# One level of Strassen's scheme for the last matrix product of a fused retention and MLP kernel

## The chip, the cores and the metric

The kernel runs on one core of one Trainium2 chip. The metric is the device time of one launch in microseconds (us), as the median of several runs. A core has five engines that run side by side, each with its own instruction queue that it works off in order: PE (TensorE, the matrix multiplier; PEld is its weight load), DVE (VectorE), ACT (ScalarE), POOL (GpSimd) and SP (SyncE, which here only issues DMAs). SBUF is the on-chip memory. PSUM is the memory that PE writes its products to; this kernel uses it as eight banks of 128 partitions by 512 float32 numbers.

## The reference: what is computed

Two layers follow each other. The first is a recurrent retention over 4 batches, 8 heads, 768 steps and a head size of 64; the second is an MLP over its 3072 rows.

```python
def _attn_ref(q, k, v):
    ...
    for t in range(S):
        state = gamma[None, :, None, None] * state + np.einsum('bhd,bhe->bhde', k[:, :, t], v[:, :, t])
        y[:, :, t] = scale * np.einsum('bhd,bhde->bhe', q[:, :, t], state)

def _moe_ref(x, w_in, w_out):     # x: 3072 x 512, w_in: 512 x 2048, w_out: 2048 x 512
    h = x @ w_in
    g = h * np.cos(h)
    return (g @ w_out).astype(np.float32)
```

All matmuls of the kernel take bf16 operands and add up in float32.

## The kernel before

**Tiles and stages.** The sequence is cut into chunks of 128 steps. A pair `p` (0 to 11) is one chunk of two batches, so 256 rows of the MLP. Two pairs make a group `g` (0 to 5) of 512 rows. For each pair there is a block: `y_block(p)`, many small matmuls that make the retention's output `y` of this pair, bring its state `st_ps` up to date and make the score matrices of pair `p + 1`. Behind it stand the block's copies: `y_copy` (two of them, ACT, to `xt`), `s_copy` (the state from PSUM to the bf16 tile `stb`) and four `a_mask` (DVE, scores times mask, to `am`). For each group there are two large products. The first, here called F, is `f_mm(g, f)` for 16 row blocks `f` of the hidden layer: four matmuls of 512 columns each into one bank; then `f_cos` (ACT, the cosine into one of three `cosb` tiles), then `f_mul` (DVE, h times cos(h), into row `f` of `gt[g % 2]`). The second, here called O, is `o_mm(g, j, part)`: for each of the four row tiles `j` of 128 rows there are 16 matmuls of 512 columns, in four parts, that take `gt` as weights and `w_out_sb` as the moving operand and add up in one bank; then `o_out` (ACT, to one of four `ob` tiles) and `o_dma` (SP, a 256 KB write).

**Order.** Groups 0 and 1 and pairs 0 to 6 are placed by a planner with given costs (`Plan`); the change doesn't touch it. From group 2 on the order is written out by hand (L946 to L970). A group has 16 steps `s`. Step `s` of group `g` issues F of block `s` of this group, and beside it one part of O of the group before. At steps 3 and 11 a block follows, with its copies and `conv` (ACT and POOL bring `q`, `k`, `v` of pair `p + 2` to bf16, SP transposes them by DMA), and SP issues loads. Blocks exist in groups 2, 3 and 4 (pairs 6 to 11). The pass `g == NG` is the end: it holds O of group 5 alone, with the last row tile split into 384 and 128 columns (`last_o`).

**What is shared.** Seven PSUM banks go round in a first-in, first-out list (`Banks`): `f_mm`, `o_mm` and `y_block` (six banks: two for `y`, four for the scores) take from its head, and the program hands a bank back where its last reader is issued. PE waits on the chip until that reader is done. Between the halves of a block one other engine passes a signal on (`told`, `hop_on`, L531); from pair 6 on this is POOL. `PRE` is 5: the float32 loads `qf`, `kf`, `vf` have five buffers each, and pair `p` uses number `p % 5`.

Of the kernel before, what the change touches and what calls it, by code (L numbers as in the profile page):

```python
# [9 lines left out]
FP32 = mybir.dt.float32  # L10
BF16 = mybir.dt.bfloat16
AF = mybir.ActivationFunctionType
ALU = mybir.AluOpType
# [160 lines left out]
def kernel(  # L174
# [9 lines left out]
    nc = tc.nc  # L184
    B, H, S, D = q.shape
    C = 128
    NC = S // C
    DM = H * D
# [3 lines left out]
    KOUT = DF // 128  # L192
    NP = B // 2 * NC
    NG = NP // 2
# [4 lines left out]
    ORDER = [0, NC] + [x for x in range(1, NP) if x != NC]  # L199
# [25 lines left out]
    w_out_sb = sb([128, KOUT, DM], BF16, "w_out_sb")  # L225
    qf = [sb([128, 2, H, D], FP32, f"qf{i}") for i in range(PRE)]
    kf = [sb([128, 2, H, D], FP32, f"kf{i}") for i in range(PRE)]
    vf = [sb([128, 2, H, D], FP32, f"vf{i}") for i in range(PRE)]
    ob = [sb([128, DM], FP32, f"ob{i}") for i in range(4)]
# [7 lines left out]
    xt = [sb([128, KIN, 4 * C], BF16, f"xt{i}") for i in range(2)]  # L237
    gt = [sb([128, KOUT, 4 * C], BF16, f"gt{i}") for i in range(2)]
    cosb = [sb([128, 4 * C], BF16, f"cosb{i}") for i in range(3)]
    kx = sb([128, H, 2, D], BF16, "kx")  # L240
    vx = sb([128, 2, H, D], BF16, "vx")
    mask = [sb([128, 128], BF16, f"mask{i}") for i in range(2)]
# [11 lines left out]
    far = gtf[:, 4352:4608].bitcast(FP32)  # L254

    amf = [gtf[:, 5120 + 1024 * i : 6144 + 1024 * i].bitcast(FP32) for i in range(2)]

    def by_b(t, p):

# [15 lines left out]
    def load(eng, p, names):  # L275

        bp, c = divmod(ORDER[p], NC)
        for n in names.split():  # L280
            t, src = SRC[n[0].lower()]
            if len(n) == 1:
                t = (qb(p) if n == "Q" else kb(p)) if n in "QK" else t[p % PRE]
                eng.dma_start(  # L284
                    out=t.rearrange("p b h d -> p (b h) d"),
                    in_=src[ds(2 * bp, 2), :, ds(c * C, C), :].rearrange(
                        "b h t d -> t (b h) d"))
            elif n[1] == "s":
# [23 lines left out]
    ENG = {"D": nc.vector, "P": nc.gpsimd}  # L312

    def copy(e, out, in_):
        if e == "A":
            nc.scalar.copy(out=out, in_=in_)  # L316
        else:
            ENG[e].tensor_copy(out=out, in_=in_)  # L318
# [37 lines left out]
    held = {}  # L356
# [228 lines left out]
    def s_copy(p, e):  # L585
        copy(e, stb[(max(p, 1) + 1) % 2], st_ps)
# [3 lines left out]
    def f_mm(g, f):  # L590
        bank = held["f", g, f] = banks.take()
        for i in range(KIN):
            nc.tensor.matmul(bank, lhsT=w_in_sb[:, i, ts(f, 128)], rhs=xt[g % 2][:, i, :],  # L593
                             start=(i == 0), stop=(i == KIN - 1))

    def f_cos(key):
        cb = cosb[f_no[0] % 3]
        f_no[0] += 1
        bank = held[key]
        held[key] = (bank, cb)  # L600
        nc.scalar.activation(out=cb, in_=bank, func=AF.Sin, bias=halfpi)  # L601

    def f_mul(g, f):
        bank, cb = held["f", g, f]
        nc.vector.tensor_tensor(out=gt[g % 2][:, f, :], in0=bank, in1=cb, op=ALU.mult)  # L605
        banks.give(bank)
# [20 lines left out]
    o_no = [0]  # L627

    def o_row(g, j):
        bp, c = divmod(ORDER[2 * g + j // 2], NC)  # L630
        return (2 * bp + j % 2) * S + c * C

    def o_mm(g, j, part):
        if part == 0:
            held["o", g, j] = banks.take()
        bank = held["o", g, j]
        for f in range(4 * part, 4 * part + 4):
            nc.tensor.matmul(bank, lhsT=gt[g % 2][:, f, ts(j, 128)], rhs=w_out_sb[:, f, :],  # L638
                             start=(f == 0), stop=(f == KOUT - 1))

    def o_out(g, j, e):
        bank = held["o", g, j]
        o = ob[o_no[0] % 4]
        o_no[0] += 1
        copy(e, o, bank)
        banks.give(bank)
        held["dma", g, j] = o

    def o_dma(g, j):
        nc.sync.dma_start(out=out[ds(o_row(g, j), C), :], in_=held.pop(("dma", g, j)))  # L650

    def last_o(g, j):

        o = ob[o_no[0] % 4]
        for i, (lo, n) in enumerate(((0, 384), (384, 128))):
            bank = banks.take()
            for f in range(KOUT):
                nc.tensor.matmul(bank[:, :n], lhsT=gt[g % 2][:, f, ts(j, 128)],  # L658
                                 rhs=w_out_sb[:, f, ds(lo, n)],
                                 start=(f == 0), stop=(f == KOUT - 1))  # L660
            copy("AD"[i], o[:, ds(lo, n)], bank[:, :n])
            (nc.sync, nc.scalar)[i].dma_start(
                out=out[ds(o_row(g, j), C), ds(lo, n)], in_=o[:, ds(lo, n)])

    def idle_mm(e, n=1):
        bank = banks.take()
# [19 lines left out]
        out=dist.rearrange("p (a b) -> p a b", a=8),  # L686
        in0=far[:, :8].unsqueeze(2).to_broadcast([128, 8, 16]),
        in1=far[:, 8:24].unsqueeze(1).to_broadcast([128, 8, 16]), op=ALU.add)
# [31 lines left out]
    at = lambda tm: dict(start=0.0, free=0.0, done=tm, lat=0.0)  # L720
# [30 lines left out]
    for p in range(PL + 2):  # L751
        c = ORDER[p] % NC
# [120 lines left out]
        for u in units:  # L873
            f = u[2]
# [49 lines left out]
    def block(p):  # L924
        nxt = p + 1 < NP
        y_block(p, nxt)
        for b in range(2):
            y_copy(p, b, "A")
        if has_s(p):
            s_copy(p, "D")  # L930
        if nxt:
            for u in range(2):
                for b in range(2):
                    a_mask(p + 1, b, u)

    def conv(p):
        for b in range(2):
            conv_k(p, b, "A")
        for b in range(2):
            conv_q(p, b, "P")  # L940
        for b in range(2):
            conv_v(p, b, "P")
        for w in (1, 0):
            dma_t(p, w)

    for g in range(2, NG + 1):  # L946
        for s in range(16):
            hf, r = divmod(s, 8)
            p = 2 * (g + 1) + hf
            if g < NG:  # L950
                if g == 2 and s == 0:
                    o_mm(1, 0, 0)
                f_mm(g, s)
                f_cos(("f", g, s))
                f_mul(g, s)
            if g == NG and s == 12:
                last_o(NG - 1, 3)
                break
            if g > 2 or s > 0:
                o_mm(g - 1, *divmod(s, 4))  # L960
            if s % 4 == 3:
                o_out(g - 1, s // 4, "A")
            if p < NP and r == 3:
                block(p)
            if s % 4 == 3:
                o_dma(g - 1, s // 4)
            if p + 2 < NP and r == 3:
                conv(p + 2)
            if p + 3 < NP and s % 4 == 3:
                load(nc.sync, p + 3, "q ks" if r == 3 else "vs")  # L970


# [28 lines left out]
```

## Time and profile before

| what | value |
|---|---|
| median of three runs (lowest to highest) | 209.26 us (208.71 to 209.42) |
| span of the profiled execution, first to last instruction | 206.6 us |
| difference of the two, which lies around the span | 2.7 us |
| PE busy | 201.9 us, 98% of the span |
| DVE busy | 112.9 us, 55% |
| ACT busy | 115.1 us, 56% |
| POOL busy | 75.2 us, 36% |
| granted TensorE clock, mean | 1.000 |
| written to and read from HBM | 6.29 MB and 27.26 MB |

The profile is of one execution; the page gives its span, and no separate device time for it. A row of a group gives the line, the engine, the operation, output and inputs with their shapes, the count, the busy time and the mean duration of one. A duration is longer than the distance between two starts where instructions overlap, as matmuls do. A row of the timeline gives start, duration, engine, line and count of a run of like instructions. Group 2's hand-written steps start at about 69.6 us, those of group 3 at 101.2 us, of group 4 at 131.8 us, of group 5 at 161.9 us, and the end at 188.7 us.

### The profile page before, as it was taken

What the parts mean: (1) busy time and instruction counts of PE and PEld (TensorE: products, weight loads), DVE (VectorE), ACT (ScalarE), POOL (GpSimd) and SP (SyncE); (2) the same over time, 40 slices, a digit from 0 to 9 for tenths busy, and PEclk for the clock granted to TensorE, in tenths of its full rate; (3) what the DMA queues carried; (4) which work ended last, traced back from release to release, by engine and by line L of the source; (5) the groups of instructions that cost most, each with busy time, mean ns of one, the idle gap of its engine ahead of it and who ended that gap; (6) DMA issues with size and microseconds to landing.
All of it is one profiled execution on the core that took longest, in us unless ns stands there. A gap on an engine that the chain in (4) does not pass through costs nothing.

```text
span 206.6 us, 5235 instructions
## 1 busy us (share of the span) xinstructions
PE 201.9 (98%) x2179; PEld 108.9 (53%) x2179; DVE 112.9 (55%) x194; ACT 115.1 (56%) x193; POOL 75.2 (36%) x79
## 2 busy tenths in 40 slices
PE   7999999999999999999999999999999999999994
PEld 2547665868945545445445445445444444444442
DVE  5477899776787548338438438448442444444000
ACT  7566794859965357547547546554555553554120
POOL 8899989799985003305206105200000000000000
PEclk9999999999999999999999999999999999999999
DMA  6999999999999865886876975501101101110212
GB/s 117 172 264 201 304 242 322 252 333 278 341 332 190 199 156 150 206 210 155 190 183 157 144 198 147 156 0 56 53 1 51 51 3 51 51 51 0 105 52 102
DMA packets 59656, 32.15 MB, mean 156 GB/s; under 512 B 48752, under 2 KB 54128, under 8 KB 59632
## 3 DMA queue, kind: packets, MB, share of 16 engines
q0 software_dynamic: 15408, 15.47, 34.6%
q1 hardware_dynamic: 44080, 16.28, 31.7%
q8 instruction: 17, 0.28, 0.6%
q10 hardware_dynamic: 144, 0.07, 0.1%
q14 instruction: 7, 0.06, 0.1%
HBM read 27.26 MB, written 6.29 MB: 162 GB/s over the span
## 4 chain that ended last, share of the span: by engine, by line
PE 93%; DMA 4%; POOL 1%; issue 0%; DVE 0%; POOLq 0%; DVEq 0%
PE bank L638 39%; PE bank L593 30%; PE bank L614 10%; DMA kx<-in_k_dram 4%; PE bank L392 2%; PE bank L483 2%; PE bank L364 2%; PE bank L658 2%; PE st_ps L511 2%; PE bank L667 2%; PE bank L497 1%; POOL ks L284 1%; PE bank L434 1%; POOL qs L284 1%; PE bank L402 0%
## 5 line engine op out<-in xcount | busy, mean ns | idle before, releaser
L601 ACT ACTIVATE cosb<-bank,halfpi 128x512 bf16<-128x512 f32 x96 | 65.6, 689 | 54.1 <-PE bank L593 47.8
L638 PE MATMUL bank<-w_out_sb,gt 128*128 128x512 bf16 x368 | 91.0, 379 | 0.0
L605 DVE TENSOR_TENSOR gt<-bank,cosb 128x512 bf16<-128x512 f32 x72 | 49.1, 689 | 55.7 <-ACT cosb L601 55.7
L593 PE MATMUL bank<-xt,w_in_sb 128*128 128x512 bf16 x288 | 73.2, 379 | 0.0
L638 PEld LDWEIGHTS <-gt 128*128 128x128 bf16 x368 | 35.5, 98 | 42.3 <-DMA w_out_sb<-in_moe_w_out_dram 0.3
L593 PEld LDWEIGHTS <-w_in_sb 128*128 128x128 bf16 x288 | 27.5, 98 | 32.3
L327 POOL TENSOR_TENSOR qs<-qf,gq 128x512 bf16<-128x512 f32 x18 | 18.5, 1046 | 42.4 <-PE bank L483 32.0
L411 DVE TENSOR_TENSOR am<-bank,mask 128x512 bf16<-128x512 f32 x40 | 24.8, 681 | 3.5 <-PE bank L392 3.5
L316 ACT COPY ob<-bank 128x512 f32<-128x512 f32 (+1 forms) x24 | 14.0, 582 | 16.0 <-PE bank L638 13.9
L614 PE MATMUL bank<-xt,w_in_sb 128*128 128x256 bf16 x192 | 22.4, 273 | 0.0
L614 PEld LDWEIGHTS <-w_in_sb 128*128 128x128 bf16 x192 | 18.6, 98 | 3.3 <-DVE xt L318 0.3
L622 DVE TENSOR_TENSOR gt<-bank,cosb 128x512 bf16<-128x512 f32 x24 | 16.2, 689 | 5.6 <-ACT cosb L601 5.4
L316 ACT CAST xt<-bank 128x512 bf16<-128x512 f32 x21 | 11.4, 588 | 10.6 <-PE bank L483 10.5
L316 ACT CAST ks<-kf 128x512 bf16<-128x512 f32 x20 | 11.5, 623 | 1.9 <-DMA kf<-in_k_dram 1.9
L667 PE MATMUL bank<-zero 128*128 128x512 bf16 x35 | 11.2, 449 | 1.1 <-DVE halfpi L683 1.1
L483 PE MATMUL bank<-am,vs 64*64 64x128 bf16 (+1 forms) x320 | 10.3, 206 | 0.1
L334 POOL TENSOR_TENSOR vs<-vf,gk 128x512 bf16<-128x512 f32 x8 | 8.2, 1043 | 6.0 <-DMA vf<-in_v_dram 3.8
L284 POOL DMA_DIRECT2D vf<-in_v_dram x8 | 9.4, 1178 | 1.9 <-DVE vs L339 1.4
L339 POOL TENSOR_TENSOR vs<-vf,gk 128x512 bf16<-128x512 f32 x8 | 8.7, 1096 | 2.5 <-PE bank L483 1.3
L318 DVE CAST stb<-st_ps 128x512 bf16<-128x512 f32 x9 | 6.2, 689 | 3.4 <-PE st_ps L511 2.6
L483 PEld LDWEIGHTS <-vs 64*64 64x64 bf16 x320 | 7.8, 107 | 0.5 <-POOLq L531 0.2
L392 PE MATMUL bank<-qkt 64*64 64x128 bf16 (+1 forms) x320 | 7.9, 206 | 0.0
(66 smaller groups left out, 131.7 us busy)
## 6 DMA issues: line engine op xcount, KB each, us to landing
out_dram<-ob SPq DMA_DIRECT2D x23, 256.0 KB, 2.5
vf<-in_v_dram POOLq DMA_DIRECT2D x8, 512.0 KB, 11.7
qf<-in_q_dram POOLq DMA_DIRECT2D x6, 512.0 KB, 12.3
kf<-in_k_dram POOLq DMA_DIRECT2D x6, 512.0 KB, 12.1
w_out_sb<-in_moe_w_out_dram POOLq DMA_DIRECT2D x4, 512.0 KB, 14.1
qf<-in_q_dram SPq DMA_DIRECT2D x4, 512.0 KB, 4.8
w_in_sb<-in_moe_w_in_dram POOLq DMA_DIRECT2D x5, 256.0 KB, 8.5
kf<-in_k_dram SPq DMA_DIRECT2D x16, 64.0 KB, 3.1
```

The lines of the kernel that those rows point to most:

```text
L284: eng.dma_start(out=t.rearrange("p b h d -> p (b h) d"), in_=src[ds(2 * bp, 2), :, ds(c * C, C), :].rearrange("b h t d -> t (b h) d"))
L316: nc.scalar.copy(out=out, in_=in_)
L327: ENG[e].tensor_tensor(out=qb(p)[:, b], in0=qf[p % PRE][:, b], in1=bc(gq, ORDER[p] % NC), op=ALU.mult)
L411: nc.vector.tensor_tensor(out=am[p % 2][b][u], in0=bank.rearrange("p (a t) -> p a t", a=HP), in1=(dec[:, b] if p < 2 else mask[second(p, 0 ...
L483: m = nc.tensor.matmul(held["yp", p][b][ts(j, 64), a, lo:], lhsT=vs[p % NB][ts(r, 64), b, h, :], rhs=am[p % 2][b][h // 4][ts(r, 64), h % 4 ...
L593: nc.tensor.matmul(bank, lhsT=w_in_sb[:, i, ts(f, 128)], rhs=xt[g % 2][:, i, :], start=(i == 0), stop=(i == KIN - 1))
L601: nc.scalar.activation(out=cb, in_=bank, func=AF.Sin, bias=halfpi)
L605: nc.vector.tensor_tensor(out=gt[g % 2][:, f, :], in0=bank, in1=cb, op=ALU.mult)
L614: nc.tensor.matmul(bank[:, ts(e, 256)], lhsT=w_in_sb[:, i, ts(f + e, 128)], rhs=xt[g % 2][:, i, ts(hf, 256)], start=(i == 0 and e == 0), s ...
L622: nc.vector.tensor_tensor(out=gt[g % 2][:, f : f + 2, ts(hf, 256)], in0=bank.rearrange("p (f t) -> p f t", f=2), in1=cb.rearrange("p (f t) ...
L638: nc.tensor.matmul(bank, lhsT=gt[g % 2][:, f, ts(j, 128)], rhs=w_out_sb[:, f, :], start=(f == 0), stop=(f == KOUT - 1))
L667: nc.tensor.matmul(bank[:, : 256 * n].rearrange("p (n t) -> p n t", n=n), lhsT=zero[:, :128], rhs=zero.unsqueeze(1).to_broadcast([128, n, ...
```

## The change

O of groups 2 to 5 is done by one level of Strassen's scheme in the form with seven products and sums that are used again. The group's hidden matrix is split into halves by rows (pairs `2g` and `2g + 1`) and by the hidden index (blocks 0 to 7 and 8 to 15), and `w_out` by the hidden index and by columns (256 each). Each of the seven products is, for both batches `j`, eight matmuls of 256 columns. DVE and POOL make the operand sums: of `w_out` once, in group 2 (`w_sum`, T1 to T4), and of `gt` in every group (`g_sum`, S1 to S4), each in two halves of 1024 bf16 elements per partition. S1, S2, S4 and T1, T2, T3 lie in load buffers 2 and 3 of `qf`, `kf` and `vf`; S3 overwrites its operand in `gt`. The partial results are added up by DVE from PSUM (`add_up`, float32), with one copy by ACT ahead, and are written by four DMAs per group in runs of 1 KB (`c_dma`). F's blocks are issued in the order 0, 8, 1, 9 and so on. `s_copy` of the hand-written blocks moves from DVE to ACT. `last_o` goes.

```diff
+    T4 = sb([128, KOUT // 2, DM // 2], BF16, "T4")
+    part1 = [sb([128, 2, DM // 2], FP32, f"part{i}") for i in range(2)]
...
+    T1, T2, T3 = (halves(t[2]) for t in (qf, kf, vf))
+    S1, S2, S4 = (halves(t[3]) for t in (qf, kf, vf))
...
-    def last_o(g, j):
...
+    def w_sum(n, e, x):
+        k = ts(x, HK // 2)
+        out, a, b, op = {
+            1: (T1, w_quad(0, 1), w_quad(0, 0), ALU.subtract),
+            2: (T2, w_quad(1, 1), T1, ALU.subtract),
+            3: (T3, w_quad(1, 1), w_quad(0, 1), ALU.subtract),
+            4: (T4, w_quad(1, 0), T2, ALU.subtract)}[n]
+        ENG[e].tensor_tensor(out=out[:, k], in0=a[:, k], in1=b[:, k], op=op)
+
+    def g_sum(g, n, e, x, of=2):
+        k = ts(x, HK // of)
+        t = gt[g % 2]
+        out, a, b, op = {
+            1: (S1, quad(t, 1, 0), quad(t, 1, 1), ALU.add),
+            2: (S2, S1, quad(t, 0, 0), ALU.subtract),
+            3: (quad(t, 1, 0), quad(t, 0, 0), quad(t, 1, 0), ALU.subtract),
+            4: (S4, quad(t, 0, 1), S2, ALU.subtract)}[n]
+        ENG[e].tensor_tensor(out=out[:, k], in0=a[:, k], in1=b[:, k], op=op)
+
+    def product(g, n, j, on=None):
+        t = gt[g % 2]
+        a, b = {
+            1: (quad(t, 0, 0), w_quad(0, 0)), 2: (quad(t, 0, 1), w_quad(1, 0)),
+            3: (S4, w_quad(1, 1)), 4: (quad(t, 1, 1), T4),
+            5: (S1, T1), 6: (S2, T2), 7: (quad(t, 1, 0), T3)}[n]
...
+        for k in range(HK):
+            nc.tensor.matmul(bank[:, ts(j, HM2)], lhsT=a[:, k, ts(j, 128)], rhs=b[:, k, :],
+                             start=(on is None and j == 0 and k == 0), stop=(k == HK - 1),
+                             skip_group_check=True)
...
+    def add_up(out, n, other, js=slice(0, 2)):
+        nc.vector.tensor_tensor(out=out[:, js], in0=pbank(n)[:, js], in1=other[:, js], op=ALU.add)
...
         if has_s(p):
-            s_copy(p, "D")
+            s_copy(p, "A")
...
+    def o_step(g, s):
+        if s in (0, 1):
+            product(g, 1, s)
+            if s == 1:
+                nc.scalar.copy(out=pu[0], in_=pbank(1))
+        elif s == 3:
+            for j in range(2):
+                product(g, 2, j, on=1)
+            O[0, 0] = new_ob()
+            nc.scalar.copy(out=O[0, 0], in_=pbank(2))
+            put(2)
+        elif s in (4, 5):
+            product(g, 6, s - 4)
+            if s == 5:
+                add_up(pu[1], 6, pu[0])
+                put(6)
+        elif s in (6, 7):
...
+        elif s in (8, 9):
+            product(g, 5, s - 8)
...
+        elif s == 11:
+            for j in range(2):
+                product(g, 3, j, on=5)
+            O[0, 1] = new_ob()
+            add_up(O[0, 1], 3, pu[1])
+            put(3)
+        elif s in (12, 13):
+            product(g, 4, s - 12)
+            if s == 13:
+                O[1, 0] = new_ob()
+                add_up(O[1, 0], 4, pu[0])
+                put(4)
+
+    def sums(g, s):
+        x = 0 if s >= 12 else 1
+        n = (1, 2, 4, 3)[s % 4]
+        if n != 4:
+            g_sum(g - x, n, "D", x)
+
+    def pool_sums(g, s):
+        if s == 3:
+            if 2 <= g - 1 < NG:
+                g_sum(g - 1, 4, "P", 1)
+        elif s == 15 and g < NG:
+            g_sum(g, 4, "P", 0)
...
-    for g in range(2, NG + 1):
+    for g in range(2, NG):
         for s in range(16):
             hf, r = divmod(s, 8)
             p = 2 * (g + 1) + hf
+            f = s // 2 + 8 * (s % 2)
...
+            f_mm(g, f)
+            f_cos(("f", g, f))
+            if s < 4 and g > 2 or s >= 12:
+                sums(g, s)
+            f_mul(g, f)
+            if g > 2:
+                o_step(g - 1, s)
+            else:
...
+                if s in (4, 5, 8, 9):
+                    w_sum(1 + s // 8, "D", s % 2)
             if p < NP and r == 3:
                 block(p)
...
+            if g == 2 and r == 3:
+                for x in range(2):
+                    w_sum(3 + s // 8, "P", x)
+            pool_sums(g, s)
...
+    g = NG - 1
+    for n in (1, 2):
+        g_sum(g, n, "D", 1)
+    g_sum(g, 4, "P", 1)
+    g_sum(g, 3, "D", 1)
+    for j in range(2):
+        product(g, 1, j)
+    nc.scalar.copy(out=pu[0], in_=pbank(1))
+    for j in range(2):
+        product(g, 4, j)
...
+    o = new_ob()
+    for j in range(2):
+        product(g, 3, j)
+        add_up(o, 3, pu[1], slice(j, j + 1))
+        c_dma(g, 0, 1, o, (nc.sync, nc.scalar)[j], slice(j, j + 1))
```

More of the change, by code (lines that the diff above doesn't have):

```diff
@@ L256, with halves @@
     amf = [gtf[:, 5120 + 1024 * i : 6144 + 1024 * i].bitcast(FP32) for i in range(2)]
+    def halves(t):
+        return t.rearrange("p b h d -> p (b h d)").bitcast(BF16).rearrange(
+            "p (f m) -> p f m", f=KOUT // 2)
+    T1, T2, T3 = (halves(t[2]) for t in (qf, kf, vf))
+    S1, S2, S4 = (halves(t[3]) for t in (qf, kf, vf))
     def by_b(t, p):
@@ L650, in o_dma @@
         nc.sync.dma_start(out=out[ds(o_row(g, j), C), :], in_=held.pop(("dma", g, j)))
-    def last_o(g, j):
[L654 to L663, printed above, removed]
+    HK, HM2 = KOUT // 2, DM // 2
@@ new lines, in quad, with w_quad @@
+    def quad(t, r, c):
+        return t[:, ts(c, HK), ts(r, HM2)]
+    def w_quad(r, c):
+        return w_out_sb[:, ts(r, HK), ts(c, HM2)]
+    def w_sum(n, e, x):
[6 more added lines that the diff above has]
+        ENG[e].tensor_tensor(out=out[:, k], in0=a[:, k], in1=b[:, k], op=op)
@@ new lines, in g_sum @@
+    def g_sum(g, n, e, x, of=2):
[13 more added lines that the diff above has]
+            5: (S1, T1), 6: (S2, T2), 7: (quad(t, 1, 0), T3)}[n]
+        if on is None and j == 0:
+            held["P", n] = banks.take()
+        elif on is not None:
+            held["P", n] = held["P", on]
+        bank = held["P", n]
+        for k in range(HK):
+            nc.tensor.matmul(bank[:, ts(j, HM2)], lhsT=a[:, k, ts(j, 128)], rhs=b[:, k, :],
+                             start=(on is None and j == 0 and k == 0), stop=(k == HK - 1),
+                             skip_group_check=True)
@@ new lines, in put, with pbank, new_ob, c_dma @@
+    def put(n):
+        banks.give(held["P", n])
+    def pbank(n):
+        return held["P", n].rearrange("p (j m) -> p j m", j=2)
+    def new_ob():
+        o_no[0] += 1
+        return ob[(o_no[0] - 1) % 4].rearrange("p (j m) -> p j m", j=2)
+    def add_up(out, n, other, js=slice(0, 2)):
+        nc.vector.tensor_tensor(out=out[:, js], in0=pbank(n)[:, js], in1=other[:, js], op=ALU.add)
+    def c_dma(g, r, c, o, eng=None, js=None):
+        bp, ch = divmod(ORDER[2 * g + r], NC)
+        rows = out.rearrange("(b s) m -> s b m", b=B)[ds(ch * C, C), ds(2 * bp, 2), ts(c, HM2)]
+        if js is not None:
+            rows, o = rows[:, js], o[:, js]
+        (eng or nc.sync).dma_start(out=rows, in_=o)
@@ L665, in idle_mm @@
+    pu = part1
     def idle_mm(e, n=1):
@@ L944, in conv, with o_send @@
             dma_t(p, w)
-    for g in range(2, NG + 1):
+    O = {}
+    def o_step(g, s):
[15 more added lines that the diff above has]
+        elif s in (6, 7):
+            product(g, 7, s - 6)
+            if s == 7:
+                add_up(pu[0], 7, pu[1])
+                put(7)
+        elif s in (8, 9):
+            product(g, 5, s - 8)
+            if s == 9:
+                O[1, 1] = new_ob()
+                add_up(O[1, 1], 5, pu[0])
+        elif s == 11:
[10 more added lines that the diff above has]
+                put(4)
+    def o_send(g, s):
+        for at, k in ((4, (0, 0)), (11, (1, 1)), (13, (0, 1)), (15, (1, 0))):
+            if s == at:
+                c_dma(g, *k, O[k])
+    def sums(g, s):
[10 more added lines that the diff above has]
+    for g in range(2, NG):
         for s in range(16):
@@ L949 @@
             p = 2 * (g + 1) + hf
[L950 to L962, printed above, removed]
+            f = s // 2 + 8 * (s % 2)
@@ new lines @@
+            if g == 2 and s == 0:
+                o_mm(1, 0, 0)
+            f_mm(g, f)
[6 more added lines that the diff above has]
+            else:
+                if s > 0:
+                    o_mm(1, *divmod(s, 4))
+                if s % 4 == 3:
+                    o_out(1, s // 4, "A")
+                if s in (4, 5, 8, 9):
+                    w_sum(1 + s // 8, "D", s % 2)
@@ L963 @@
             if p < NP and r == 3:
                 block(p)
-            if s % 4 == 3:
-                o_dma(g - 1, s // 4)
+            if g == 2:
+                if s % 4 == 3:
+                    o_dma(1, s // 4)
+            else:
+                o_send(g - 1, s)
             if p + 2 < NP and r == 3:
                 conv(p + 2)
+            if g == 2 and r == 3:
+                for x in range(2):
+                    w_sum(3 + s // 8, "P", x)
+            pool_sums(g, s)
             if p + 3 < NP and s % 4 == 3:
@@ L970 @@
                 load(nc.sync, p + 3, "q ks" if r == 3 else "vs")
+    g = NG - 1
[9 more added lines that the diff above has]
+    for j in range(2):
+        product(g, 2, j, on=1)
+    o = new_ob()
+    nc.scalar.copy(out=o, in_=pbank(2))
+    put(2)
+    c_dma(g, 0, 0, o)
+    for j in range(2):
+        product(g, 6, j)
@@ new lines @@
+    add_up(pu[1], 6, pu[0])
+    put(6)
+    for j in range(2):
+        product(g, 7, j)
+    add_up(pu[0], 7, pu[1])
+    put(7)
+    o = new_ob()
+    add_up(o, 4, pu[0])
+    put(4)
+    c_dma(g, 1, 0, o)
+    for j in range(2):
+        product(g, 5, j)
+    o = new_ob()
+    add_up(o, 5, pu[0])
+    c_dma(g, 1, 1, o)
+    add_up(pu[1], 5, pu[1])
+    put(5)
+    o = new_ob()
+    for j in range(2):
+        product(g, 3, j)
+        add_up(o, 3, pu[1], slice(j, j + 1))
+        c_dma(g, 0, 1, o, (nc.sync, nc.scalar)[j], slice(j, j + 1))
@@ L974 @@
+    put(3)
 _INS = ['q', 'k', 'v', 'moe_w_in', 'moe_w_out']
```

## The prediction

> **What bounds the kernel now.** I read the page first: the engines' shares, the slices, the chain.
>
> ```profile
> span 206.6 us, 5235 instructions
> PE 201.9 (98%) x2179; PEld 108.9 (53%) x2179; DVE 112.9 (55%) x194; ACT 115.1 (56%) x193; POOL 75.2 (36%) x79
> PEclk9999999999999999999999999999999999999999
> PE 93%; DMA 4%; POOL 1%; issue 0%; DVE 0%; POOLq 0%; DVEq 0%
> ```
>
> PE is busy 98% of the time at full clock and carries 93% of the chain that ends last, so time comes only from fewer PE columns. But a busy share is a mean; the second view, busy time by stage, cuts the stretch that the change touches: groups 2, 3, 4, 5 and the end.
>
> ```profile
> core 0: us, PE busy (x) PEld busy (x) DVE busy (x) ACT busy (x) POOL busy (x), PEclk, DMA share, GB/s
> 71.40:101.20 29.80, 29.80 (x349) 14.65 (x348) 17.28 (x27) 16.68 (x27) 8.17 (x8) 1.00 0.72 177
> 101.20:131.80 30.60, 30.60 (x354) 14.93 (x353) 16.88 (x26) 17.30 (x29) 8.18 (x8) 1.00 0.77 173
> 131.80:161.90 30.10, 29.97 (x289) 14.21 (x288) 13.97 (x21) 15.24 (x24) 0.00 (x0) 1.00 0.10 36
> 161.90:188.70 26.80, 26.80 (x126) 12.13 (x125) 11.07 (x16) 12.70 (x20) 0.00 (x0) 1.00 0.10 40
> 188.70:206.60 17.90, 14.87 (x85) 7.53 (x83) 0.98 (x2) 3.51 (x6) 0.00 (x0) 1.00 0.20 75
> ```
>
> In the first four stages length and PE time agree within 0.13 us: PE has no gap to lose or to fill. DVE and ACT have 12 us or more free in each of them, POOL 21 us. Third, PE's timeline, for the true distance of matmuls:
>
> ```profile
> 48.40 7.15 PE L614 MATMUL bank<-xt,w_in_sb 128*128 128x256 bf16 x64
> 188.69 11.39 PE L638 MATMUL bank<-w_out_sb,gt 128*128 128x512 bf16 x52
> ```
>
> A matmul of 512 columns costs (11.39 - 0.38) / 51 = 0.2159 us, one of 256 columns (7.15 - 0.27) / 63 = 0.1092 us (0.38 and 0.27 are the single durations of these groups). Half the columns cost 50.6%: the weight load (98 ns in both groups) hides behind either.
>
> **The change on PE.** O of a group was 4 x 16 matmuls of 512 columns, 64 x 0.2159 = 13.82 us. Now it is 7 products x 2 batches x 8 = 112 matmuls of 256 columns, 112 x 0.1092 = 12.23 us. Four groups: 4 x 1.59 = 6.37 us. The split last tile goes too: 3.66 us from its first start to its end, against 16 x 0.2159 + 0.16 (what a matmul's duration exceeds its distance by) = 3.61: 0.05 more. Together -6.42 us, all on the path. Blocks and F keep their matmuls; F's new order only makes row halves ready sooner.
>
> **The end.** The last result was 128 columns copied by DVE in 0.29 us and a 64 KB write; it becomes an `add_up` of 256 columns, 0.29 + 128 x 1.02 ns = 0.42 (slope: 0.293 us at 128 columns, 0.686 at 512, both of DVE's two-input rows), and a 128 KB write (to landing: 1.7 us for 64 KB, 1.8 for 192 KB). +0.18 us. Ahead of it: after the last `f_mul` DVE still makes the second halves of S1 and S2, 1.2 us, and POOL that of S4, 2.1 us. Products 1, 4 and 2 (5.2 us of PE) cover S1 and S2, and 6, 7 and 5 (another 5.2) cover S4.
>
> **DVE, ACT and POOL.** The rows to cost them by:
>
> ```profile
> L605 DVE TENSOR_TENSOR gt<-bank,cosb 128x512 bf16<-128x512 f32 x72 | 49.1, 689 | 55.7 <-ACT cosb L601 55.7
> L327 POOL TENSOR_TENSOR qs<-qf,gq 128x512 bf16<-128x512 f32 x18 | 18.5, 1046 | 42.4 <-PE bank L483 32.0
> L318 DVE CAST stb<-st_ps 128x512 bf16<-128x512 f32 x9 | 6.2, 689 | 3.4 <-PE st_ps L511 2.6
> L318 DVE COPY qkt<-bank 128x512 bf16<-128x512 bf16 x11 | 4.4, 417 | 3.1 <-PE bank L364 3.1
> 94.88 2.47 DVE L411 TENSOR_TENSOR am<-bank,mask 128x512 bf16<-128x512 f32 x4
> ```
>
> Five `add_up` per group are like L605, 0.69 us, and in a queue one per 0.60 us (four masks in 2.47). Off DVE go two state copies per group with a block, to ACT, which loses two of four output copies: ACT is even. The operand sums, six halves per group on DVE, have no row: two bf16 inputs and a bf16 output in SBUF, 1024 elements. Bounds: at one element per 1.02 ns 0.69 + 512 x 1.02 = 1.21 us; at twice that rate 0.69 us. The nearest row is the `qkt` copy, 16 bits in and out: 0.417 against 0.681 us for the same copy from float32, so the 16-bit form does run faster. I take 0.69 (0.60 in a queue) and keep 1.21 (1.13). By the Trainium skill ("VectorE: DVE Perf Modes", the perf-mode tier table) `tensor_tensor` on bf16 in SBUF runs at twice the base rate; no run here shows that form, and the sum by it would be the one with 0.69.
>
> DVE in group 3 then: 16.9 + 5 x 0.6 + 6 x 0.6 - 1.2 = 22.3 us, of a stage of 30.6 - 1.6 = 29.0. It fits as a mean, so the question is the local queue. It is fullest from the block at step 11 on, where four masks, three sums and an `add_up` meet two short PE steps (14 and 15 have no product). Count from the start E of F behind that block (94.31 in the profile; masks may start 0.3 ahead of it, as at 69.34 ahead of 69.62). PE per step: F 0.864, one product and batch 0.873. Group 3 to 4, everything at 0.6 in a queue: masks end 2.1; S1 2.7; cosine 12 is late, since ACT's block copies and casts end at 2.7 (before: 2.16, plus `s_copy` 0.5), so `f_mul` of step 12 ends 4.0; S2 4.6; `f_mul` 13 5.2; `add_up` 5.8; `f_mul` 14 6.4. Product 1 starts at 6.05 and its eighth matmul, the one that needs `f_mul` 14, at 6.8: 0.4 spare. On: S3 7.0, `f_mul` 15 7.6, S1 8.2, `f_mul` 0 8.8, S2 9.4, `f_mul` 1 10.0, `f_mul` 2 11.0 (its cosine ends 10.4), S3 11.6, `f_mul` 3 12.2. PE reaches the next block at 12.1 and the bank of step 3's F, the block's last score bank, some 0.7 later (scores start 0.38 into the block at 62.23): 0.6 spare. Group 2 to 3 has 1.7 us more room (there O is still whole) and no `add_up`; group 4 to 5 has no masks. So nothing stalls, if DVE waits for nobody.
>
> It may wait for POOL, the wait that the change adds. Before, DVE had no two-input operation from SBUF beyond 64.1 us; earlier there is this meeting:
>
> ```profile
> 58.68 0.68 DVE L339 TENSOR_TENSOR vs<-vf,gk 128x512 bf16<-128x512 f32 x1
> 58.92 1.34 POOL L339 TENSOR_TENSOR vs<-vf,gk 128x512 bf16<-128x512 f32 x1 [0.78 <-PE bank L392]
> ```
>
> POOL began 0.24 us into DVE's operation and took 1.34 us, where its like take 1.04 to 1.07: 0.3 lost. The reverse, DVE second, the trace doesn't show. Bounds: DVE loses nothing; or it loses what is left of POOL's operation in front. The Trainium skill ("SBUF — State Buffer", section Who interferes with whom) speaks against the change here: a DVE instruction with two SBUF inputs and a POOL instruction that reads SBUF exclude each other, and the later one waits for the whole of the earlier; the row agrees for POOL, and by the rule the upper bound would hold, with 204.7 for the sum. A POOL half sum, 1024 elements, is by rows 2 x 1.05 = 2.1 us (2.5 by the slow L423, 1.27 us). Group 3 to 4: POOL's `conv_v` runs from E + 3.5 to 5.5 (128.37 against E = 124.83), so S2 (due 4.0) may start 0.6 to 1.6 late; POOL's S4 follows S2 for 2.1 us and holds S3 another 0.3 to 0.7. That is 0.9 to 2.3 us against 0.6 spare: 0.3 to 1.7 of stall. Group 2 to 3: POOL has `conv_v` to 5.0, both halves of T4 and S4, to 11.3; S2 then waits to 11.3 and `f_mul` 3 ends at 14.3, against 12.8 + 1.7 = 14.5: none. I take 0.6 us of stalls in all, near the lower end, since the lower end needs only that DVE gets in between POOL's two operations; range 0 to 1.7.
>
> Edits at nothing: `w_sum`, four DVE halves in steps with 1.03 us idle each, and its wait for POOL's `conv_q` of pair 7, over by 62.5; POOL's signal in the block (L531), queued behind T4 and S4, which end at 11.3 where the block comes at 13.9 (without that room, each us of POOL more is a us of PE); SP's `c_dma`, in place of `o_dma` behind results that are a step old; and product 2's wait for ACT's copy of product 1, with two F steps between, 1.7 us against 0.8. If that cover goes, each costs its own lateness, four times at most.
>
> **The sum.** Against the profile: 206.6 - 6.42 + 0.18 + 0.6 = 201.0. The median is 2.7 above the span, outside the kernel: 203.6 us.
>
> **Rivals.** *DVE's sums run at one element per 1.02 ns.* Six at 1.13 put `f_mul` 3 of group 3 to 4 at 14.3, with 12.8 needed: 1.5 us; with the waits for POOL up to 3. Result 204.5 to 206.0, middle 205.3. For it: no row of that form; against: the `qkt` row. *POOL holds DVE, and it ends slower.* One mechanism: POOL's half sums, a form without a row, last longer than 2.1 us, DVE's sums wait behind them, `f_mul` behind the sums, and the block's score bank behind `f_mul`. At 3 us each, group 2 to 3: POOL ends at 14, S2 14.6, `f_mul` 3 17.0, 2.5 lost; group 3 to 4: S4 to 8.6, `f_mul` 3 14.0, 1.2 lost: 206.7. At 4 us: 5.5 + 2.2 = 7.7 lost, 210.7. It decides from about 3.6 us on, 1.7 times what the rows give. Against: the 1.046 us row is steady (18 of them, 18.5 us busy). *The products' matmuls keep more distance than 0.109.* Break-even is 13.82 / 112 = 0.1234 us; for it, their weights come from tiles that DVE and POOL have just written; against, L614 also reads weights of 128 columns with a new set each time, at 0.1092. At 0.122 the time is 209.
>
> **The numbers.** Forecast case 0.66 (202.8 to 204.9: stalls 0 to 1.7, give and take 0.2); slow sums 0.19; POOL holding DVE beyond 3.6 us a sum 0.12, slower; wide distance 0.03, the same. What a measurement of this kernel can tell from no change is about 0.3%, 0.6 us. Faster 0.66 + 0.19 = 0.85; same 0.03; slower 0.12. The range, 202.6 to 207.0, takes in the first two cases and the milder waits for POOL, and leaves out the 0.12 and 0.03 and a little.
>
> **What would show it.** Right: product groups of 128x256 on PE at 0.109; stages of groups 3, 4, 5 and the end 1.6 us shorter each; the sums near 0.69 on DVE; PE idle under 2 us from group 3 on. Wrong: PE waiting for `gt` or for a score bank behind a block; DVE idle "issue" ahead of the sums while POOL works; POOL rows of 1024 elements over 3.6 us; the weight load as the releaser ahead of the products.

## The result, and the profile after

| | before | after |
|---|---|---|
| median of 4 runs each | 208.99 us (208.39 to 209.42) | 205.56 us (204.86 to 206.35) |
| ratio of the times, 95% interval | | 0.9835 [0.9801, 0.9869] |
| span of the profiled execution | 206.6 us | 203.0 us |

The change makes the kernel 1.65% faster, 3.4 us, where 5.7 were forecast. One execution of run e2 below ran at a granted clock of 0.757 and took 256.41 us; it is left out of that run's median. The profile after is of the execution of 204.86 us. The page of the changed kernel first:

```profile
span 203.0 us, 5642 instructions
PE 193.9 (96%) x2331; PEld 126.4 (62%) x2355; DVE 146.6 (72%) x238; ACT 112.8 (56%) x190; POOL 102.7 (51%) x91
PEclk9999999999999999999999999999999999999999
L691 POOL TENSOR_TENSOR vf<-gt,kf 128x1024 bf16<-128x1024 bf16 x8 | 17.8, 2220 | 48.4 <-DVE kf L691 41.6
```

PE's work fell by 8.0 us of busy time, the span by 3.6, at the same clock: PE now stands still somewhere. (This trace lacks some matmul records: 2331 matmuls stand against 2355 weight loads, and gaps of 0.21 us, just one matmul, show at the same places in several runs. So PE's shares are a little low and the 8.0 too high, and below I compare starts.) Busy time by stage, here groups 3, 4, 5 and the end:

```profile
101.25:131.20 29.95, 28.92 (x398) 19.65 (x401) 23.91 (x32) 16.81 (x29) 16.10 (x12) 1.00 0.66 160
131.20:160.12 28.92, 28.33 (x334) 18.92 (x337) 21.47 (x34) 14.66 (x24) 6.21 (x3) 1.00 0.18 56
160.12:186.15 26.03, 25.82 (x173) 17.22 (x176) 17.62 (x27) 12.17 (x19) 4.27 (x3) 1.00 0.12 41
186.15:203.00 16.85, 12.60 (x112) 10.77 (x111) 8.09 (x13) 1.89 (x4) 2.59 (x2) 1.00 0.22 79
```

Divided at the same places (the starts of F of step 0 at 101.23, 131.75 and 161.92, and the end of the last step of group 5 at 189.55), the stages of before are 30.52, 30.17, 27.63 and 17.05 us. Group 5 gained 1.60 us, all that was forecast for a group; group 4 gained 1.25, group 3 only 0.57, and the end only 0.20. Three places in PE's timeline hold what is missing. First the rows of before that they are compared with, the two around the block of pair 8 and the last one:

```profile
107.27 1.03 PE L638 MATMUL bank<-w_out_sb,gt 128*128 128x512 bf16 x4
...
109.54 1.04 PE L593 MATMUL bank<-xt,w_in_sb 128*128 128x512 bf16 x4
...
199.91 3.66 PE L658 MATMUL bank<-w_out_sb,gt 128*128 128x384 bf16 x32
```

And after:

```profile
106.45 1.91 PE L707 MATMUL bank<-w_out_sb,gt 128*128 128x256 bf16 x16
...
110.07 0.24 PE L401 MATMUL bank<-qkt 64*64 64x128 bf16 x2 [0.82 <-DVE gt L614]
...
110.62 1.04 PE L602 MATMUL bank<-xt,w_in_sb 128*128 128x512 bf16 x3
...
132.06 0.93 PE L707 MATMUL bank<-w_out_sb,gt 128*128 128x256 bf16 x7
133.14 0.28 PE L707 MATMUL bank<-w_out_sb,gt 128*128 128x256 bf16 x1 [0.15 <-DVE gt L614]
...
196.69 1.04 PE L707 MATMUL bank<-w_out_sb,vf 128*128 128x256 bf16 x8
198.74 1.03 PE L707 MATMUL bank<-w_out_sb,vf 128*128 128x256 bf16 x8 [1.02 <-DVE ob L722]
```

The first group ends its 16 starts at 106.45 + 16 x 0.109 = 108.20, and F behind the block starts at 110.62: the block of pair 8 takes 2.42 us, before 1.40 (107.27 + 4 x 0.216 = 108.13, to 109.54). Inside, a score matmul waits for `f_mul` (L614), because it needs that bank: 1.02 lost. Product 1 of group 3 waits 0.31 for `f_mul` of step 14: its eighth matmul was due at 132.06 + 7 x 0.109 = 132.83 and starts at 133.14 (the row's own figure is smaller, since a matmul's modelled end lies behind its start distance). And the very last eight matmuls start 1.18 us after the eight before them are through (196.69 + 8 x 0.109 = 197.56), held by an addition of DVE (`add_up`, L722). Together 2.5 us.

Why `f_mul` was late ahead of the block of pair 8 is seen on DVE and POOL in that stretch:

```profile
98.31 0.71 DVE L691 TENSOR_TENSOR kf<-qf,gt 128x1024 bf16<-128x1024 bf16 x1
...
100.24 2.32 DVE L691 TENSOR_TENSOR gt<-gt 128x1024 bf16<-128x1024 bf16 x1
102.48 0.68 DVE L614 TENSOR_TENSOR gt<-bank,cosb 128x512 bf16<-128x512 f32 x1
103.26 1.82 DVE L691 TENSOR_TENSOR qf<-gt 128x1024 bf16<-128x1024 bf16 x1
...
105.61 2.01 DVE L691 TENSOR_TENSOR kf<-qf,gt 128x1024 bf16<-128x1024 bf16 x1
...
109.34 0.68 DVE L614 TENSOR_TENSOR gt<-bank,cosb 128x512 bf16<-128x512 f32 x1
...
198.26 0.42 DVE L722 TENSOR_TENSOR ob<-bank,part 128x256 f32<-128x256 f32 x1
```

```profile
97.44 2.49 POOL L343 TENSOR_TENSOR vs<-vf,gk 128x512 bf16<-128x512 f32 x2 [1.39 <-DMA vf<-in_v_dram]
99.89 4.65 POOL L679 TENSOR_TENSOR T<-w_out_sb,kf 128x1024 bf16<-128x1024 bf16 x2
104.50 2.57 POOL L691 TENSOR_TENSOR vf<-gt,kf 128x1024 bf16<-128x1024 bf16 x1
```

In this stretch an operand sum of DVE takes 0.68 to 0.71 us where it finds POOL idle or gets in between two of its operations, and 1.8 to 2.3 where it begins behind an operation of POOL; it then ends some 0.55 us after that operation. Where less of POOL's operation was left, less was lost (1.23 and 1.09 us at 130.06 and 133.01). `f_mul`, with one input from PSUM, takes 0.68 in the same stretch. `f_mul` of step 3 ends at 110.02, and the scores go on just then. The last row of DVE is the addition that stands between the two halves of the last product.

### The profile page after: what moved, and what is told of

The parts are those of the page before. It is cut to its first block, busy times and chain, and to the rows that moved or that the text cites. A ratio compares the mean times of both kernels' runs of the same rounds, so it can differ in the third digit from the quotient of the medians.

```text
span 203.0 us, 5642 instructions
## 1 busy us (share of the span) xinstructions
PE 193.9 (96%) x2331; PEld 126.4 (62%) x2355; DVE 146.6 (72%) x238; ACT 112.8 (56%) x190; POOL 102.7 (51%) x91
## 5 line engine op out<-in xcount | busy, mean ns | idle before, releaser
L602 PE MATMUL bank<-xt,w_in_sb 128*128 128x512 bf16 x271 | 68.8, 379 | 0.9 <-issue 0.3
L614 DVE TENSOR_TENSOR gt<-bank,cosb 128x512 bf16<-128x512 f32 x72 | 49.0, 687 | 26.1 <-ACT cosb L610 26.0
L691 POOL TENSOR_TENSOR vf<-gt,kf 128x1024 bf16<-128x1024 bf16 x8 | 17.8, 2220 | 48.4 <-DVE kf L691 41.6
L647 PE MATMUL bank<-w_out_sb,gt 128*128 128x512 bf16 x121 | 30.2, 379 | 0.6 <-issue 0.5
L707 PEld LDWEIGHTS <-gt 128*128 128x128 bf16 x256 | 25.0, 98 | 8.2 <-DVE gt L614 0.6
L647 PEld LDWEIGHTS <-gt 128*128 128x128 bf16 x128 | 12.0, 98 | 14.2 <-DMA w_out_sb<-in_moe_w_out_dram 0.5
L325 ACT CAST xt<-bank 128x512 bf16<-128x512 f32 x21 | 11.4, 588 | 15.6 <-PE bank L492 15.6
L707 PE MATMUL bank<-w_out_sb,gt 128*128 128x256 bf16 x128 | 16.0, 273 | 0.2 <-DVE gt L614 0.2
L737 PE MATMUL bank<-zero 128*128 128x512 bf16 x35 | 10.7, 436 | 1.1 <-DVE halfpi L753 1.1
L343 POOL TENSOR_TENSOR vs<-vf,gk 128x512 bf16<-128x512 f32 x8 | 9.1, 1157 | 4.5 <-DMA vf<-in_v_dram 4.5
L722 DVE TENSOR_TENSOR ob<-bank,part 128x512 f32<-128x512 f32 (+1 forms) x13 | 8.4, 646 | 2.6 <-PE bank L707 2.5
L348 POOL TENSOR_TENSOR vs<-vf,gk 128x512 bf16<-128x512 f32 x8 | 8.4, 1053 | 3.4 <-PE bank L492 1.9
```

What stands on the lines that cost most here:

```text
L691: ENG[e].tensor_tensor(out=out[:, k], in0=a[:, k], in1=b[:, k], op=op)
L707: nc.tensor.matmul(bank[:, ts(j, HM2)], lhsT=a[:, k, ts(j, 128)], rhs=b[:, k, :], start=(on is None and j == 0 and k == 0), stop=(k == HK ...
L737: nc.tensor.matmul(bank[:, : 256 * n].rearrange("p (n t) -> p n t", n=n), lhsT=zero[:, :128], rhs=zero.unsqueeze(1).to_broadcast([128, n, ...
```

## Experiments

Times differ by up to 1 us between runs of one kernel already ahead of group 2, where PE waits for the first loads (1.0 us for `w_in_sb` in e7, none in the profile after). So beside the median I give the **path**: from the start of F of step 4 in group 2, right behind the block of pair 6, to the end of the last product (its last start group plus 0.109 per matmul). It is 124.4 us before (78.99 to 203.40) and 120.6 after (78.99 to 199.61). Each path and each wait below comes from one profile; the two profiles of the changed kernel, after and e7, differ by 0.5 us in their paths.

| kernel | median | ratio to before, 95% | path | block of pair 8 | product 1 of group 3 waits | block of pair 10 | last wait |
| --- | --- | --- | --- | --- | --- | --- | --- |
| after | 205.56 | 0.9835 [0.9801, 0.9869] | 120.6 | 2.42 | 0.31 | 1.42 | 1.18 |
| e7, the same | 205.4 | 0.9834 [0.981, 0.9857] | 120.1 | 2.00 | 0 | 1.64 | 1.19 |
| e1, two last banks | 204.2 | 0.9764 [0.9734, 0.9795] | 119.7 | 2.80 | 0 | 1.64 | 0 |
| e2, T4 later | 204.43 | 0.9756 [0.9723, 0.9789] | 119.8 | 1.41 | 0.53 | 1.41 | 1.19 |
| e3, sums on DVE | 204.52 | 0.9768 [0.9739, 0.9797] | 119.7 | 1.48 | 0.30 | 1.42 | 1.18 |
| e4, no sums of `gt` | 203.99 | 0.9743 [0.9716, 0.9771] | 119.3 | 1.47 | 0 | 1.41 | 1.18 |
| e5, state on DVE | 206.0 | 0.9855 [0.9831, 0.9879] | 121.2 | 2.69 | 0.66 | 1.40 | 1.19 |
| e6, both cures | 203.42 | 0.9732 [0.9706, 0.9758] | 118.7 | 1.50 | 0.57 | 1.41 | 0 |
| e9, e6 again | 203.53 | 0.9744 [0.9715, 0.9772] | 118.2 | 1.41 | 0.03 | 1.42 | 0 |
| e8, e6 and later addition | 203.45 | 0.9736 [0.9711, 0.9761] | 118.5 | 1.41 | 0 | 1.70 | 0 |

Before, the blocks of pairs 8 and 10 took 1.41 us each. The intervals of e1, e2 and e3 lie below that of the changed kernel, if narrowly.

**e1: a bank for each half of the last product.**

```diff
-    def product(g, n, j, on=None):
+    def product(g, n, j, on=None, first=False):
...
-                             start=(on is None and j == 0 and k == 0), stop=(k == HK - 1),
+                             start=((first or on is None and j == 0) and k == 0), stop=(k == HK - 1),
...
     for j in range(2):
-        product(g, 3, j)
+        held["P", 3] = banks.take()
+        product(g, 3, j, on=3, first=True)
         add_up(o, 3, pu[1], slice(j, j + 1))
         c_dma(g, 0, 1, o, (nc.sync, nc.scalar)[j], slice(j, j + 1))
-    put(3)
+        put(3)
```

> The changed kernel, but the two halves of the very last product get a PSUM bank each instead of sharing one. Bank theory: PE's 1.02 us wait ahead of the last eight matmuls comes only from the shared bank (DVE still reads the first half when PE wants to write the second), so it goes: the end (from the last F to the last instruction) 16.85 -> 15.8 us, span 203.0 -> 202.0. Rival, late DVE: PE or the result waits for DVE's queue of final additions in any case, and the last addition still starts near 199.8; span stays at 203.0. Stages of groups 3 to 5 unchanged in both.

The end of PE's and DVE's timelines in e1:

```profile
197.20 1.91 PE L707 MATMUL bank<-w_out_sb,vf 128*128 128x256 bf16 x16
...
198.01 0.68 DVE L722 TENSOR_TENSOR part<-bank,part 128x512 f32<-128x512 f32 x1
198.78 0.79 DVE L722 TENSOR_TENSOR ob<-bank,part 128x256 f32<-128x256 f32 x2
```

All sixteen matmuls run on without a break, and the two additions follow each other. The end took 15.6 us (15.8 were expected, 16.85 in the profile after). The bank theory holds: PE waited to write the second half of a bank whose first half DVE had yet to read. Whether the chip needs this wait or only the program's bookkeeping sets it, no run here shows. DVE's queue is part of the price: in the profile after it reached the first half 0.5 us late (198.26, where the last matmul's modelled end is 197.73), behind two other additions. The path lost 0.96 us and not 1.18: in this run the blocks of pairs 8 and 10 came out 0.38 and 0.22 longer, and product 1 of group 3 did not wait (0.31). The span, 202.3 and not 202.0, also began its path 0.3 us later.

**e2: T4 one block later.**

```diff
-            if g == 2 and r == 3:
+            if g == 2 and s == 3:
                 for x in range(2):
-                    w_sum(3 + s // 8, "P", x)
+                    w_sum(3, "P", x)
             pool_sums(g, s)
+            if g == 3 and s == 3:
+                for x in range(2):
+                    w_sum(4, "P", x)
```

> The changed kernel, but POOL makes T4 at step 3 of group 3 instead of step 11 of group 2, so that it no longer runs beside DVE's sums of group 2. The count of operations on every engine is unchanged. Hold theory (a DVE sum and a POOL operation from SBUF exclude each other, and the wait for POOL makes f_mul 3 late for the block): DVE's sums between 96 and 109 us come to 0.7 us each but for at most one held by S4, the block of pair 8 takes 1.4 us instead of 2.4, group 3 is 1.0 us shorter (29.95 -> 29.0), span 202.0. Rival, load theory (DVE simply has too many operations between two blocks): DVE has the same operations, so the block stays at 2.4 us and the span at 203.0.

DVE in e2, the sums of group 2 from the third on, and POOL's one half sum beside them:

```profile
100.75 2.31 DVE L691 TENSOR_TENSOR gt<-gt 128x1024 bf16<-128x1024 bf16 x1
...
103.76 0.69 DVE L691 TENSOR_TENSOR qf<-gt 128x1024 bf16<-128x1024 bf16 x1
...
104.97 0.68 DVE L691 TENSOR_TENSOR kf<-qf,gt 128x1024 bf16<-128x1024 bf16 x1
```

```profile
100.39 2.12 POOL L691 TENSOR_TENSOR vf<-gt,kf 128x1024 bf16<-128x1024 bf16 x1
```

Just as many operations on DVE, and the block of pair 8 is back at 1.41 us. The one sum that began 0.36 us behind a POOL operation took 2.31, the two after it 0.69 and 0.68. Load theory is out for this block; hold theory gave 1.4 and stands. The path came out 0.8 us shorter, not 1.0, since product 1 of group 3 waited 0.53 here; the span, with other waits ahead of group 2, only 0.3 (202.7, where 202.0 was expected).

**e3: all operand sums on DVE.**

```diff
-                    w_sum(3 + s // 8, "P", x)
+                    w_sum(3 + s // 8, "D", x)
...
-                g_sum(g - 1, 4, "P", 1)
+                g_sum(g - 1, 4, "D", 1)
...
-            g_sum(g, 4, "P", 0)
+            g_sum(g, 4, "D", 0)
...
-    g_sum(g, 4, "P", 1)
+    g_sum(g, 4, "D", 1)
```

> The changed kernel, but all operand sums are on DVE: T3, T4 and S4 too, at the same places of the order. DVE gets 12 more operations of 0.6 to 0.7 us, three of them between the blocks of pairs 7 and 8. Hold theory: with POOL doing only q and v, the sums take 0.7 us, f_mul 3 of group 3 is ready in time, and the block of pair 8 takes 1.4 to 1.6 us instead of 2.4; group 4's first block may lose 0.4. Span 202.0 to 202.6. Load theory: 1.8 us more DVE work between the two blocks makes the block of pair 8 later still, 2.4 -> 4.2 us, and the span 204.8 or more.

```profile
103.89 0.68 DVE L691 TENSOR_TENSOR vf<-gt,kf 128x1024 bf16<-128x1024 bf16 x1
104.49 0.68 DVE L691 TENSOR_TENSOR qf<-gt 128x1024 bf16<-128x1024 bf16 x1
105.09 0.68 DVE L614 TENSOR_TENSOR gt<-bank,cosb 128x512 bf16<-128x512 f32 x1
```

In DVE's timeline the sum that POOL needed 2.1 us for takes 0.68, one per 0.60 in a queue. Three operations more between the blocks of pairs 7 and 8, and that block takes 1.48 us, not 4.2: this is the clearest case against load theory. The span, 202.8, lies 0.2 above what was given (this run's path began 0.8 us later than in the profile after), and the 0.4 feared for group 4's first block did not come there; product 1 of group 3 waits 0.30 instead. Two engines that exclude each other do less together here than the faster one alone: in the profile after, six half sums and two `f_mul` took from 99.89 to 107.62, 7.7 us; eight operations of DVE at 0.60 in a queue would be 4.8, an estimate.

**e4: products without sums.** The kernel leaves out S1 to S4, so its result is not the product; only its time is of use.

```diff
     def g_sum(g, n, e, x, of=2):
...
-        ENG[e].tensor_tensor(out=out[:, k], in0=a[:, k], in1=b[:, k], op=op)
+        pass
...
-            3: (S4, w_quad(1, 1)), 4: (quad(t, 1, 1), T4),
-            5: (S1, T1), 6: (S2, T2), 7: (quad(t, 1, 0), T3)}[n]
+            3: (quad(t, 0, 1), w_quad(1, 1)), 4: (quad(t, 1, 1), T4),
+            5: (quad(t, 1, 1), T1), 6: (quad(t, 1, 0), T2), 7: (quad(t, 1, 0), T3)}[n]
```

> The changed kernel without the sums of gt (S1 to S4 are left out, and the products 3, 5 and 6 read halves of gt instead; all 28 products' matmuls, w_out's sums and the additions stay). It asks what the products alone bring. Theory: PE's stalls behind f_mul go, and the last product's bank wait of 1.02 us stays: group 3 is 28.93 us, group 4 28.6, group 5 26.0, span 203.0 - 1.0 - 0.33 - 0.05 = 201.6. Rival, wide distance: if the products' matmuls themselves kept more than 0.109 us (their weights not freshly written here), groups 3 to 5 would each get shorter by more than the stalls named, also group 5, and the span would fall below 201.

The path is 119.3 us, 5.1 below before; with the last wait of 1.18 taken off, 6.3 of the 6.42 that the prediction counted on PE. Groups 3 and 4 take 29.0 and 28.6 us, as expected. Wide distance is out: group 5 stays at 26.0 us. The span was 202.6 and not 201.6, a miss of the expectation: this run reached the start of the path 0.9 us later than the profile after.

**e7 and e6: the yardstick, and both cures together** (e1's and e3's edits).

> The changed kernel once more, unaltered, as the yardstick for the two runs beside it. PE's path from F of step 4 in group 2 (start right behind the block of pair 6) to the end of the last product: 120.6 us in the first profile of it, 124.4 in the kernel before. All theories: 120.3 to 121.0 here, the block of pair 8 between 2.2 and 2.9 us long, and the wait of about 1.0 us ahead of the last eight matmuls; ratio to the kernel before 0.980 to 0.987.

> The changed kernel with both cures: all operand sums on DVE, and a PSUM bank for each half of the last product. Hold theory with bank theory: the two losses stand in different stages and add up, so the path from F of step 4 in group 2 to PE's end is 120.6 - 1.0 (block of pair 8) - 0.3 (product 1 of group 3) - 1.2 (last product) = 118.2 us, some 1% faster than the changed kernel and 3% faster than the kernel before (ratio 0.969 to 0.974). Rival, hidden late work: with both waits gone another is next (DVE's queue ahead of the last additions, or S4 ahead of product 3), and not more than 1.5 us of the 2.4 come off.

e7's path came out 0.2 us below what was given for it, and its block of pair 8 at 2.00 us, where 2.2 to 2.9 were given: POOL's loads arrived later, so its T4 met other sums. e6 and its repetition e9 have paths of 118.7 and 118.2, in the mean 1.9 below the mean of the two runs of the changed kernel; medians 2.0 us below e7. The interval of e6, [0.9706, 0.9758], lies below that of the changed kernel, [0.981, 0.9857]. The two cured losses do add up: e9 meets the 118.2 that was given, and e6 misses it by 0.5 because product 1 of group 3 waits 0.57 in it. The expectation had counted that wait among the cured, wrongly: what holds S2 there is POOL's `conv_v` (S2 takes 1.49 us in e6), and that stays on POOL. The rival's late work, DVE's queue ahead of the last additions or S4 ahead of product 3, did not come forward.

**e5: the state copy back on DVE.**

```diff
-            s_copy(p, "A")
+            s_copy(p, "D")
```

> The changed kernel with one part undone: the state copy behind each block is on DVE again instead of ACT. It asks what that part carries. Queue theory (DVE between two blocks with masks has no room left): each state copy puts 0.60 us more ahead of f_mul 3, so the block of pair 8 goes from 2.4 to 2.8 or 3.0 us, product 1 of group 3 waits 0.9 instead of 0.3 and the block of pair 10 little or nothing: path from F of step 4 in group 2 to PE's end 121.4 to 122.0 instead of 120.6. Rival: the cosine is what comes last behind a block (ACT is 0.5 us earlier here), so the two cancel and the path stays within 0.3 of 120.6.

The path is 121.2 us, 0.6 and 1.2 above the two runs of the changed kernel; block of pair 8 2.69 us, product 1 waits 0.66. The sign is the queue theory's, and its bounds were 0.2 too high. With one profile of e5, and 0.5 us between the two of the changed kernel, this is a hint and not shown; the medians don't show it either, for the intervals overlap.

**e8: the addition behind `f_mul`, and e9 beside it** (on top of e6).

```diff
             product(g, 4, s - 12)
-            if s == 13:
-                O[1, 0] = new_ob()
-                add_up(O[1, 0], 4, pu[0])
-                put(4)
+        elif s == 14:
+            O[1, 0] = new_ob()
+            add_up(O[1, 0], 4, pu[0])
+            put(4)
```

> All sums on DVE and a bank for each half of the last product, and in addition DVE's addition of product 4 stands behind f_mul of step 14 instead of ahead of it. Queue theory for the wait in product 1 of group 3 (f_mul 14 is late because everything that DVE has ahead of it adds up): f_mul 14 ends 0.6 us earlier, the wait (0.57 us in the run with the two cures) goes, and the path from F of step 4 in group 2 to PE's end is 118.71 - 0.57 = 118.1 to 118.2 us; ratio to the kernel before 0.968 to 0.973. Rival, the cosine: f_mul 14 waits for ACT there, and the order on DVE changes nothing, path 118.7.

> The run with the two cures once more as yardstick for the run beside it: path from F of step 4 in group 2 to PE's end 118.2 to 118.8 us, ratio 0.970 to 0.976 under all theories.

The edit did its work at product 1, and the path gained nothing by it. In e8 S2 took 1.40 us beside `conv_v`, nearly as in e6 (1.49); `f_mul` 14 ended at 132.42, ahead of the 132.59 at which product 1 needs it, with no idle time of DVE ahead of it, and PE did not wait. So the rival, the cosine, is out for this wait. e9, without the edit, waits only 0.03, but there S2 met less of `conv_v` (1.05 us). What e8 saved came back in the block of pair 10, 1.70 us long: PE reached it sooner, and its last score bank hung on `f_mul` 3, which ended 1.1 us after the block's start (139.02 and 137.92). In e6 `f_mul` 3 ended 0.6 us after the block's start and cost nothing; in e1 and e7, with 1.64, it ended 1.0 after it. DVE's queue up to `f_mul` 3 is as long with the edit as without, and where it is late, PE meets it in one place or the other. The path, 118.5, missed the 118.1 to 118.2 given, and the ratio lies just above its bound. The wait in product 1 came in five of the ten profiles (0.30 to 0.66 us), and goes with when `conv_v` gets its load.

## Why the prediction was right, and what it mis-sized

Direction and range were right: the kernel is faster, as forecast, and 205.56 lies between 202.6 and 207.0. The gain was 3.4 us of 5.7. Of the 2.3 missing, 1.9 are stalls, 2.5 us and not 0.6; the rest is within what two profiles of one kernel differ by. There is luck in it: the likeliest case by itself reached from 202.8 to 204.9, and 205.56 lies outside that, among the times given to slow sums on DVE, which did not come. What broke that case is a wait that the prediction did not have at all, at the very end (below): with that wait gone, e1 measures 204.2. The stalls behind POOL, 1.02 and 0.31, lie within the 0 to 1.7 that it gave. One of its own signs of being wrong also showed, PE waiting for `gt` and for a score bank behind a block, and PE's waits from group 3 on came to 2.5 us, where it gave under 2.

- **The products: right.** 0.109 us per matmul of 256 columns ((1.91 - 0.27) / 15), 1.60 us gained in group 5, 6.3 us in all by e4, against 6.42. (In the sum, 4 x 1.59 is 6.36 and not 6.37.)
- **What lies around the span: wrong, without harm.** The 2.7 us is a median less the span of one execution. Wherever the runs have time and span of the same execution, the two differ by 1.7 to 1.9, so the profiled one took some 208.4 us, an estimate. The forecast time is in effect the median of before less 5.6, so it does not change.
- **The end's last step: right.** The addition of 256 columns took 0.43 us (0.42 forecast), and from PE's end to the span's end it is 3.4 us against 3.2, +0.2 (+0.18). **The end before it: a wait that was overlooked.** The prediction priced the final addition and listed what the products wait for, not what waits for an addition. Both halves of the last product share a bank, and the addition of the first stands between them (198.26 in DVE's timeline, 0.42 us long): 1.18 us, where the sum had nothing.
- **DVE's sums: right in the choice.** 0.68 us alone, the 0.69 that was taken. That is twice the rate of `f_mul`, 0.689 us for 512 elements with one input from PSUM, and the case of 1.21 us is out. The Trainium skill ("VectorE: DVE Perf Modes", the perf-mode tier table) states the same: `tensor_tensor` runs at twice the base rate on bf16 in SBUF and at the base rate from PSUM.
- **The wait for POOL: mechanism right, size wrong.** The prediction gave 0 for group 2 to 3, with `f_mul` 3 at 14.3 and 14.5 needed. It came at 15.7 (110.02 less 94.33): 1.02 lost. The term that failed is POOL's own timetable. It let POOL end at 11.3; it ended at 12.7 (107.07). POOL was held by DVE too: T4's halves took 4.65 us, in e2 without sums beside them 4.20; `conv_v` took 2.49 and not 2.04; S4 2.57 and not 2.12. A hold counted on one side only leaves out the other side's loss. Here the trace of before had shown that very side, the 1.34 us of L339. For group 3 to 4 the prediction gave 0.3 to 1.7, at `f_mul` 3 and the block of pair 10, and put no hold on `f_mul` 14, with 0.4 spare for product 1. The 0.31 fits in size, not in place: S2, held by `conv_v` (1.23 us), made `f_mul` 14 late and product 1 waited, while the block took its 1.42. In e7, the same kernel, it is the block that is 0.2 longer. The rule of the Trainium skill ("SBUF — State Buffer", Who interferes with whom), that the later of the two waits for the whole earlier one, agrees with 2.32, 1.82 and 2.01 us, and with the 0.68 of `f_mul`, which has only one input from SBUF.
- **The slower rival** needed POOL sums of 3.6 us. They took 2.12 alone (2.1 by the rows) and 2.57 at worst. Its mechanism was at work at the size of the first case.
- **`w_sum` at nothing**: T1 and T2 cost nothing, T4 was what POOL's timetable broke on.

## What to carry to other kernels

Cutting PE's columns pays in full (here 6.3 of 6.4 us) where PE is the bound, if what feeds the new products fits beside the old work; so look for the stretch where the helping engine's queue is fullest, and count there. Where two engines exclude each other, let the faster one do all of it, or keep them apart in time; giving work to the idle engine made both slower here. At the very end, give each part of the last result its own PSUM bank, so that reading one doesn't hold up the next (1.18 us here).

## What the runs showed of the hardware

DVE's two-input operation on bf16 in SBUF takes 0.68 us for 1024 elements per partition, POOL's 2.12. Beside each other, DVE's took up to 2.41 and POOL's up to 2.57; between two POOL operations in its queue DVE got its turn (100.24 to 102.56 while T4's two halves ran from 99.89 to 104.54). POOL loses time as DVE does, some 0.45 us per meeting with a sum (2.57 against 2.12, 4.65 against 4.20); the prediction's timetable for POOL had left this out.
